# Fourteen TensorE products of a tile of ones ahead of the first real product of a fused attention and token-mixing kernel

## Chip, cores and metric

The kernel runs on one core of one Trainium2 chip. The metric is device time in microseconds. The kernel before took 584.02 us, the median of three runs (583.85, 584.02 and 584.76 us).

## What is computed

Two blocks follow one another for eight batch entries: banded attention with 8 heads of width 64 over 576 positions, then a mixing block on the 512 columns that the heads give together.

```python
scores = q @ k.T / sqrt(64)        # heads 0-3: the last 32 positions
                                   # heads 4-7: every 4th of the last 128
x = softmax(masked scores) @ v     # to [8, 576, 512]
theta = x @ w_theta
y = w_tok_r @ (x * cos(theta)) + w_tok_i @ (x * sin(theta))
u = x + y
out = u + relu(u @ w_ch)
```

## The kernel before

Heads are taken in pairs, four pairs to a batch entry. The host lays out q, k and v so that a pair's masked scores are 9 strips of 128 rows by 64 columns. For each pair, in a batch entry:

- **scores** (L441): the strips are computed in two halves, of 5 and of 4 strips, each into one of two PSUM banks tagged "s". In the first entry, L424 first writes the mask into the bank (an identity in bf16 times the mask tile), then L468 adds two f32 products of 64 columns per strip, 10 in the first half and 8 in the second (each is two rows of the trace, so x20 and x16). DVE takes the row maximum (L430) and subtracts it (L433), which frees the bank. ACT computes exp (L493), DVE the row sums (L495) and their reciprocal (L507, L508), POOL multiplies (L510).
- **flip** (L543, first entry only): TensorE transposes the probabilities (L561), DVE and ACT copy them out (L536, L539). Later entries use DVE transposes (`turn`, L525).
- **pv** (L603): probabilities times v (L617) into the bank pair tagged "v" (one buffer, 1024 f32 columns), copied out by ACT (L581).

Then `theta0` and `theta` (L667, L685) multiply by w_theta, `trig` makes sine and cosine (K L787 to cos L705) and splits the products with x into a high and a low part (L644, L646), `token` (L850) and `chan` (L882) do the two large products in three passes each, and DVE, ACT and POOL make the residuals. Weights come in packed and are unpacked by DVE and ACT (`unpack`, L332 to L342) and split by ACT and POOL (`split`, L350, L352).

What sets the order. All TensorE instructions are kept in the order in which the program writes them (the helper `pe`, L170). For the first batch entry, a planner in the kernel (class `Order`) also orders DVE, ACT, POOL and the DMA issues, with ranks and estimated costs; from L987 on (`od.live = False`, batch entries 1 to 7 of the last stages and 2 to 7 of the first) only TensorE's order is written by hand, and a scheduler at build time orders the other engines with its own simulated clock.

All loads are issued by SP in one queue. `first_loads` (L270) brings the mask and the bf16 identity, then q and k of the four pairs of the first entry with the f32 identity after pair 0, then v of the four pairs; then come w_theta (L325) and the token weights (L323, L325). `consts` (L301) sets a constant on DVE (L303) and clears two tiles on POOL (L307). In the kernel before, TensorE's first instruction is the mask product L424 of pair 0.

The last lines ahead of the planner's start, next to which the change is made:

```python
    UH = {d: reserve(f"u{d}") for d in range(NC)}
    od.live = True
    go(first_loads(), 0)
    go(consts(), 0)
```

Of the kernel before, what the change touches and what calls it, by code (L numbers as in the profile page):

```python
# [8 lines left out]
F32 = mybir.dt.float32  # L9
F32R = mybir.dt.float32r  # L10
BF16 = mybir.dt.bfloat16
# [7 lines left out]
DM = H * D  # L19
# [18 lines left out]

FG0 = {4: ("zl2", "zl6"), 0: ("zl3", "zl7"), 1: ("zh3", "zh7")}
COS_PSUM, SIN_PSUM = True, True  # L40
KORD = (0, 4, 1, 5, 2, 6, 3, 7, 8)
TP0 = {4: "s", 0: "s", 1: "x", 2: "t", 3: "s"}
TP = {4: "t", 0: "s", 1: "s", 2: "t", 3: "s"}
# [18 lines left out]
class Order:  # L62
# [20 lines left out]
    def go(self, gen, rank=None):  # L83
        if not self.live:
            for _ in gen:
                pass
            return
        self.serial += 1
        t = [self.rank if rank is None else rank, self.serial, self.now, gen, None, 0.0]
        self.tasks.append(t)  # L90
        self.advance(t)
# [60 lines left out]
def build(ctx, tc, qT, kT, vw, wth, wtk, wch, maskb, ident, identb, outT):  # L152
    nc = tc.nc
    cp = ctx.enter_context(tc.tile_pool(name="const", bufs=1))
# [7 lines left out]
    ps_v = ctx.enter_context(tc.tile_pool(name="ps_v", bufs=1, space=PSUM))  # L162
# [7 lines left out]
    def pe(ins):  # L170
        tc.keep_in_program_order(ins)
# [13 lines left out]
    def reserve(tag):  # L185
        taken[tag] = taken.get(tag, -1) + 1
        return taken[tag]

    def take(tag, bufs, n=None):
        n = reserve(tag) if n is None else n  # L190
        if od.live:
            if n >= bufs:
                yield None, ("free", tag, n - bufs)
            if n:
                yield None, ("got", tag, n - 1)
            signal(("got", tag, n))
        return n
# [5 lines left out]
    def bank(tag, name):  # L203
        if tag == "v":
            n = yield from take(tag, 1)
            return ps_v.tile([128, 2 * DM], F32, tag=tag, name=name), (tag, n)
        pl, bufs = banks[tag]
        n = yield from take(tag, bufs)
        return pl.tile([128, DM], F32, tag=tag, name=name), (tag, n)
# [60 lines left out]
    def first_loads():  # L270
        yield "DMA", dma(3 * BW + 64)
        pin(nc.sync.dma_start(mskb, maskb.bitcast(BF16)))
        pin(nc.sync.dma_start(idb, identb.bitcast(BF16)))
        for pr in range(NP):
            yield from take(f"xh{pr}", 1, 0)
            yield from take(f"u{pr}", 1, 0)
            pqs.append(hp.tile([128, 2, S], F32R, tag=f"xh{pr}", name=f"P0_{pr}").bitcast(F32)[:, 0])
            q = hp.tile([128, 2, S], F32R, tag=f"u{pr}", name=f"q0_{pr}").bitcast(F32)
            q = q.rearrange("p a b -> p (a b)").rearrange("p (a b) -> p a b", b=2 * QB)
            k = first_k[:, KE * pr:KE * pr + KE]  # L280
            yield "DMA", dma(2 * S)
            pin(nc.sync.dma_start(q, qT[0, pr]))
            yield "DMA", dma(KE)
            pin(nc.sync.dma_start(k, kT[0, pr]))
            qks[0, pr] = (q, k, None)
            if pr == 0:
                yield "DMA", dma(128)
                pin(nc.sync.dma_start(idt, ident))
            signal(("qk", 0, pr))
        for pr in range(NP // 2):  # L290
            v = first_v[:, NJ * 128 * pr:NJ * 128 * pr + NJ * 128].rearrange("p (a b) -> p a b", b=128)
            yield "DMA", dma(NJ * 128)
            pin(nc.sync.dma_start(v, vw[0, pr]))
            for h, t in (("a", v[:, :VA]), ("b", v[:, VA:])):
                vs[h, 0, pr] = (t, None)
                signal(("v" + h, 0, pr))
        for pr in range(NP // 2, NP):
            yield from load_va(pr)
            yield from load_vb(pr)
# [517 lines left out]
    def residual(b, d, g, ps, rel):  # L817
        ts = slice(HS * g, HS * g + HS)
        x = xf[b, d]
        if g == 0:  # L820
            yield from take(f"u{d}", 1, UH.get(d) if b == 0 else None)
            u = hp.tile([128, 2, S], F32R, tag=f"u{d}", name=f"u{b}_{d}")
# [10 lines left out]
    def unit_bank(b, n):  # L833
        return "mmx"[n % 3] if b else "m"

    def token(b, d, g):
        yield None, ("z", b, KORD[0])
        yield None, ("wtk", g, KORD[0] // 2)
        ps, rel = yield from bank(unit_bank(b, NC * g + d), f"y{b}_{d}_{g}")
        ps = ps[:, :HS]  # L840
        cs = slice(128 * d, 128 * d + 128)
        n = 0
        for kt in KORD:
            yield None, ("z", b, kt)
            yield None, ("wtk", g, kt // 2)
            zh, zl = zs[b, kt]
            wh, wl = (w[:, HS * (kt % 2):HS * (kt % 2) + HS] for w in wtks[g, kt // 2])
            yield "PE", 369
            for l, r in ((zh, wh), (zh, wl), (zl, wh)):
                pe(nc.tensor.matmul(ps, l[:, cs], r, start=(n == 0), stop=(n == 3 * NK - 1)))  # L850
                n += 1
        signal(("tk", b, d, g))
        go(residual(b, d, g, ps, rel), RANK["evacuate"])
# [99 lines left out]
    EA, LA, LA2 = ([(t, reserve(t)) for t in ts] for ts in (EARLY, LATE, LATE2))  # L953
    XH = {p: reserve(f"xh{p}") for p in range(NP)}
    UH = {d: reserve(f"u{d}") for d in range(NC)}
    od.live = True
    go(first_loads(), 0)
    go(consts(), 0)
# [100 lines left out]
```

## Time and profile before

| | |
|---|---|
| three runs, median | 584.02 us |
| profiled execution, its own time | 585.12 us |
| its span, first to last instruction | 583.3 us |
| mean granted TensorE clock of the span | 0.987 |
| TensorE busy | 553.4 us, 95% |
| VectorE (DVE) busy | 377.9 us, 65% |
| ScalarE (ACT) busy | 343.9 us, 59% |
| GpSimd (POOL) busy | 222.5 us, 38% |

The profiled execution took 1.8 us more than its span, for what lies around the first and the last instruction, and 1.10 us more than the median of the three runs. Busy times overlap between engines. A busy TensorE need not run at its full clock: the profile gives the clock granted by the throttle as a share, 1.00 for 2.4 GHz and 0.50 for 1.2 GHz, from the first change of the clock that it recorded.

### The profile page before, as it was taken

What the parts mean: (1) busy time and instruction counts of PE and PEld (TensorE: products, weight loads), DVE (VectorE), ACT (ScalarE), POOL (GpSimd) and SP (SyncE); (2) the same over time, 40 slices, a digit from 0 to 9 for tenths busy, and PEclk for the clock granted to TensorE, in tenths of its full rate; (3) what the DMA queues carried; (4) which work ended last, traced back from release to release, by engine and by line L of the source; (5) the groups of instructions that cost most, each with busy time, mean ns of one, the idle gap of its engine ahead of it and who ended that gap; (6) DMA issues with size and microseconds to landing.
All of it is one profiled execution on the core that took longest, in us unless ns stands there. A gap on an engine that the chain in (4) does not pass through costs nothing.

```text
span 583.3 us, 13997 instructions
## 1 busy us (share of the span) xinstructions
PE 553.4 (95%) x5464; PEld 503.5 (86%) x5464; DVE 377.9 (65%) x1156; ACT 343.9 (59%) x939; POOL 222.5 (38%) x206
## 2 busy tenths in 40 slices
PE   5997799999999899999999899998999899999997
PEld 3744698879999799988999799988999799989997
DVE  3779798866666768666765767666775667545112
ACT  1498967767554784459555695349645685267110
POOL 2227855525124362326324263225423262326120
PEclk9999699899999999999999999999999999999999
DMA  8990437601748056460746246470746323331002
GB/s 300 400 360 16 172 101 247 212 0 75 215 144 200 25 175 211 100 174 27 261 144 162 65 144 202 116 197 1 251 146 165 96 83 102 66 98 60 24 0 82
DMA packets 45586, 81.91 MB, mean 140 GB/s; under 512 B 3920, under 2 KB 19024, under 8 KB 45520
## 3 DMA queue, kind: packets, MB, share of 16 engines
q1 hardware_dynamic: 45520, 81.02, 43.9%
q8 instruction: 43, 0.70, 0.5%
q14 instruction: 23, 0.19, 0.1%
HBM read 64.49 MB, written 16.52 MB: 139 GB/s over the span
## 4 chain that ended last, share of the span: by engine, by line
DVE 31%; PE 29%; ACT 26%; POOL 6%; issue 4%; DMA 3%; SPq 1%; ACTq 0%; DVEq 0%
DVE pt L525 14%; PE y L850 13%; ACT P L504 10%; PE c L882 7%; PE th L685 4%; DVE P L409 4%; POOL zl L646 3%; DVE xh L599 2%; POOL P L510 2%; ACT zh L644 2%; ACT K L698 2%; ACT K L787 2%; PE s L468 2%; ACT cos L705 2%; ACT th L796 2%
## 5 line engine op out<-in xcount | busy, mean ns | idle before, releaser
L830 POOL TENSOR_TENSOR u<-x,u 128x288 fp32r<-128x288 f32 x64 | 54.9, 858 | 190.1 <-ACT u L828 190.1
L525 DVE STREAM_TRANSPOSE pt<-P 32x288 f32<-32x288 f32 x224 | 105.1, 469 | 12.1 <-POOL P L510 8.5
L882 PE MATMUL c<-u,late_wc 128*128 128x288 f32 x768 | 108.9, 295 | 0.0
L882 PEld LDWEIGHTS c<-u,late_wc 128*128 128x128 f32 x768 | 105.9, 188 | 2.8
L850 PE MATMUL y<-wtkh,zh 128*128 128x288 f32 x288 | 90.4, 314 | 1.8 <-ACT zh L644 1.8
L828 ACT CAST u<-x 128x288 fp32r<-128x288 f32 x64 | 27.4, 429 | 108.0 <-DVE x L825 108.0
L850 PE MATMUL y<-wtkh,zl 128*128 128x288 f32 x288 | 86.4, 300 | 4.0 <-POOL zl L646 4.0
L646 POOL TENSOR_TENSOR zl<-g,zh 128x512 fp32r<-128x512 f32 x40 | 52.6, 1317 | 94.8 <-ACT zh L644 81.9
L850 PE MATMUL y<-wtkl,zh 128*128 128x288 f32 x288 | 86.0, 299 | 0.0
L685 PE MATMUL th<-wthh,xh 128*128 128x512 f32 x224 | 75.1, 396 | 7.4 <-DVE g L748 7.4
L504 ACT ACTIVATE P<-P,mx 128x64 f32<-128x64 f32 x216 | 72.0, 335 | 10.3 <-DVE mx L498 9.6
L850 PE MATMUL y<-late_wt_b,zh 128*128 128x288 f32 x320 | 68.2, 297 | 0.0
L825 DVE TENSOR_TENSOR x<-y,x 128x288 f32<-128x288 f32 x64 | 28.6, 450 | 54.9 <-PE y L850 54.6
L850 PEld LDWEIGHTS y<-wtkh,zh 128*128 128x128 f32 x288 | 55.3, 192 | 5.3 <-ACT zh L644 2.9
L850 PEld LDWEIGHTS y<-wtkh,zl 128*128 128x128 f32 x288 | 55.3, 192 | 4.7 <-POOL zl L646 4.7
L685 PEld LDWEIGHTS th<-wthh,xh 128*128 128x128 f32 x224 | 42.0, 187 | 17.3 <-issue 8.4
L850 PE MATMUL y<-late_wt_a,zh 128*128 128x288 f32 x256 | 56.8, 304 | 0.0
L850 PEld LDWEIGHTS y<-wtkl,zh 128*128 128x128 f32 x288 | 55.3, 192 | 0.3 <-issue 0.3
L510 POOL TENSOR_TENSOR P<-P,sm 128x576 f32<-128x576 f32 x32 | 37.5, 1172 | 42.0 <-DVE sm L508 18.1
L850 PEld LDWEIGHTS y<-late_wt_b,zh 128*128 128x128 f32 x320 | 51.5, 189 | 0.3
L850 PE MATMUL y<-late_wt_b,zl 128*128 128x288 f32 x160 | 47.3, 296 | 0.0
L581 ACT COPY x<-o 128x576 f32<-128x576 f32 x32 | 29.7, 928 | 28.8 <-PE o L617 24.0
(108 smaller groups left out, 1107.6 us busy)
## 6 DMA issues: line engine op xcount, KB each, us to landing
q<-in_qT_dram SPq DMA_DIRECT2D x32, 576.0 KB, 5.1
va<-in_vw_dram SPq DMA_DIRECT2D x30, 320.0 KB, 3.4
k<-in_kT_dram SPq DMA_DIRECT2D x28, 304.0 KB, 5.7
out_dram<-x SPq DMA_DIRECT2D x28, 288.0 KB, 2.3
vb<-in_vw_dram SPq DMA_DIRECT2D x29, 256.0 KB, 3.8
xd<-xq SPq DMA_DIRECT2D x24, 288.0 KB, 5.2
xn<-xd SPq DMA_DIRECT2D x24, 256.0 KB, 5.1
st_wtk<-in_wtk_dram SPq DMA_DIRECT2D x8, 576.0 KB, 9.1
```

Of the source, the lines that this page charges most:

```text
L409: pin(nc.vector.tensor_tensor_reduce(out=P[:, n], in0=ps[:, n - g0], in1=mskb[:, mask_of(pr, n)], op0=ALU.add, op1=ALU.max, scale=1.0, sca ...
L504: table(nc.scalar.activation(P[:, n], P[:, n], AF.Exp, bias=mx[:, n:n + 1], scale=SCALE, accum_out=sm[:, n:n + 1]))
L510: pin(nc.gpsimd.tensor_tensor(P, P, sm.unsqueeze(2).to_broadcast([128, NJ, BW]), op=ALU.mult))
L525: pin(nc.vector.transpose(pmats[b, pr][k0:k0 + QB, :, hh, QB * e:QB * e + QB], P[p0:p0 + QB, :, QB * o:QB * o + QB]))
L581: pin(nc.scalar.copy(dst, src))
L646: pin(nc.gpsimd.tensor_tensor(lo, z, hi.bitcast(F32), op=ALU.subtract))
L685: pe(nc.tensor.matmul(pt, l, r, start=(n == 0), stop=(n == 3 * NC - 1)))
L825: pin(nc.vector.tensor_tensor(x[:, ts], ps, x[:, ts], op=ALU.add))
L828: pin(nc.scalar.copy(uh[b, d][:, ts], x[:, ts]))
L830: pin(nc.gpsimd.tensor_tensor(ul[b, d][:, ts], x[:, ts], uh[b, d][:, ts].bitcast(F32), op=ALU.subtract))
L850: pe(nc.tensor.matmul(ps, l[:, cs], r, start=(n == 0), stop=(n == 3 * NK - 1)))
L882: pe(nc.tensor.matmul(ps, l[:, cs], r[:, ts], start=(n == 0), stop=(n == 3 * NC - 1)))
```

## The change

A tile of ones, 128 partitions by 512 columns in bf16, is made by a DVE memset. Fourteen products of it (128 x 128 stationary, 512 columns moving) are written into the first bank of the "v" bank pair, one over the other. They are issued through `pe`, so they stand ahead of every other TensorE instruction. Nothing reads what they write. Everything else is unchanged.

```diff
+WARM_UP = 14
...
     UH = {d: reserve(f"u{d}") for d in range(NC)}
+
+    ones = cp.tile([128, DM], BF16, name="ones")
+    nc.vector.memset(ones, 1.0)
+    busy = ps_v.tile([128, 2 * DM], F32, tag="v", name="busy")
+    for n in range(WARM_UP):
+        pe(nc.tensor.matmul(busy[:, :DM], ones[:, :128], ones, start=True, stop=True))
     od.live = True
     go(first_loads(), 0)
     go(consts(), 0)
```

## Rows read from the trace of the kernel before

**Rows 1.** The page, busy time of each engine: us, share of the span, instructions.

```profile
PE 553.4 (95%) x5464; PEld 503.5 (86%) x5464; DVE 377.9 (65%) x1156; ACT 343.9 (59%) x939; POOL 222.5 (38%) x206
```

**Rows 2.** Busy time by stretch: us from:to, length, engines (instructions), clock, DMA share, GB/s.

```profile
13.38:19.10 5.72, 5.72 (x86) 4.98 (x86) 3.07 (x8) 1.10 (x2) 1.15 (x1) 1.00 1.03 404
19.10:56.00 36.90, 33.48 (x378) 19.07 (x376) 32.04 (x69) 29.17 (x51) 15.85 (x11) 1.00 0.66 252
...
120.00:580.00 460.00, 451.53 (x4313) 423.93 (x4311) 283.04 (x929) 262.55 (x722) 161.95 (x153) 1.00 0.40 120
```

**Rows 3.** The chain that ended last, 3 to 24 us: start, length, what.

```profile
3.53 6.73 DMA first_k<-in_kT_dram
...
10.40 1.35 PE s L468 x20
...
13.38 0.45 PE s L424 x5
13.83 1.27 PE s L468 x20
15.10 0.33 PE s L424 x4
15.42 1.05 PE s L468 x16
16.48 1.26 PE pT L561 x20
17.74 0.38 PE s L424 x5
18.12 1.07 PE pT L561 x16
...
21.32 0.80 PE pT L561 x20
22.11 0.22 PE s L424 x4
22.34 0.64 PE pT L561 x16
```

**Rows 4.** The timeline, 0 to 25 us: start, length, engine, line, operation, form, idle before.

```profile
0.73 2.05 POOL L307 MEMSET pt<- 128x1152 f32 x2 [0.29 <-POOLq L1045]
...
0.80 0.06 DVE L303 MEMSET halfpi<- 128x1 f32 x1 [0.80 <-PEq L1045]
...
7.79 0.49 DVE L430 TENSOR_REDUCE mx<-s 128x5 f32<-128x320 f32 x1 [6.93 <-PE s L468]
...
19.10 0.82 PE L468 MATMUL s<-first_k,q 128*64 128x64 f32 x20
...
24.41 0.91 DVE L332 TENSOR_SCALAR st_wth<-st_wth 128x512 f32<-128x512 f32 x1
```

**Rows 5.** DMA issues at 5.5 and at 11.7 us: queue, count, KB, us to landing.

```profile
first_k<-in_kT_dram SPq DMA_DIRECT2D x1, 304.0 KB, 9.2
...
st_wth<-in_wth_dram SPq DMA_DIRECT2D x1, 512.0 KB, 8.7
```

**Rows 6.** TensorE products at either clock: lines of 67.8 to 73.7, timeline of 47.

```profile
L850 PE MATMUL y<-wtkh,zl 128*128 128x288 f32 x8 | 3.7, 462 | 1.1 <-POOL zl L646 1.1
...
47.04 3.77 PE L667 MATMUL th<-st_wth,x 128*128 128x512 f32 x8
```

**Rows 7.** Busy time by stretch around the recorded changes of the clock; columns as rows 2.

```profile
56.00:60.14 4.14, 1.50 (x21) 1.11 (x20) 4.14 (x9) 3.47 (x8) 3.71 (x4) 1.00 0.63 163
60.14:63.55 3.41, 3.38 (x41) 2.96 (x42) 2.64 (x21) 3.39 (x6) 3.41 (x4) 0.50 0.86 331
63.55:66.96 3.41, 1.45 (x8) 0.99 (x8) 3.41 (x14) 3.34 (x13) 2.43 (x3) 1.00 0.71 241
66.96:73.79 6.83, 5.92 (x24) 5.92 (x25) 4.55 (x11) 6.83 (x31) 6.20 (x6) 0.50 0.03 12
...
328.00:332.00 4.00, 2.50 (x12) 1.97 (x11) 1.96 (x3) 3.89 (x8) 0.04 (x1) 1.00 0.00 0
```

## The prediction, made before the change was run

> **What bounds the kernel now.** The page comes first: TensorE is busy 95% of the span [rows 1]. Such an average mixes stages, so the busy times by stretch are read next. From 120 to 580 us TensorE is busy 451.5 of 460 us, at the full clock: that part is a queue of products, and whatever starts it earlier ends it earlier. From 19.1 to 56 us VectorE (32.0 of 36.9 us) and ScalarE (29.2) are the crowded ones, passing work to each other. From 13.4 to 19.1 TensorE is busy in every moment, with VectorE half idle [rows 2]. The third view, the chain that ended last, says who holds whom at the start: the load of pair 1's k until 10.3 us, then a chain that is TensorE almost throughout until 19.2: scores of pairs 1 and 2, their masks, the flips of pair 0 [rows 3].
>
> The reader should next compare equal work on both sides of 19.1. Twenty rows of score products take 1.35 and 1.27 us in the chain at 10.4 and 13.8, and 0.82 us at 19.10 in the timeline; the flip of 20 rows takes 1.26 at 16.5 and 0.80 at 21.3 [rows 3, 4]. Nothing but the clock differs, so TensorE runs at the lower of its two levels (1.2 GHz) until about 19.1 us and at 2.4 GHz after it. The clock column shows 1.00 before 19.1 too [rows 2]; the durations contradict it, and I go by them. Before this rise TensorE had been busy without a break for 5.7 us.
>
> **The change, part by part.** The loads don't move: SP issues them as before, and none of their queue waits for TensorE until far behind the first products.
>
> *The memset.* VectorE does one 59 ns memset at 0.80 and then nothing until 7.79 us [rows 4]. No VectorE memset of 512 columns is in the trace. The bounds are that small one, 0.06 us, and the 512-column VectorE operation at 24.41, 0.91 us; I take 0.46 us from POOL's memsets (2.05 us for two of 1152 columns, so 0.89 ns a column) [rows 4]. It is hidden, and sets when the products can begin: about 1.4 us.
>
> *Fourteen products.* No bf16 product of 512 columns is in the trace. At the lower clock 24 one-pass products of 288 columns fill 5.92 us [rows 7], 0.247 us each and 0.86 ns a column, or 0.44 us for 512. The bounds: half of that, if the clock were full at once, so 3.1 us in all; and twice the f32 row of 512 columns (8 rows in 3.77 us at the full clock, 0.47 each [rows 6]), so 0.94 at the lower and 13.2 us in all. The first is excluded for most of them, as the clock starts low; the bf16 product is one pass like the 288-column one, which is the nearer row. Fourteen take 6.1 us if all run low, and TensorE is free at about 7.5; if the clock rises on the way, at about 6.5. The Trainium skill ("TensorE: Matmul & The Clock Gate", section "Wait — 56ns, not 53.3ns?") gives 426.7 ns for such a product at the lower clock; by it the fourteen take 5.97 us.
>
> *Pair 0.* Its mask products, which ran at 3.0 us, and its scores (from 6.41 us, when k had landed) now stand behind the fourteen. They would be done by 7.5 + 0.22 + 0.82 + 0.22 + 0.64 = 9.4 us at full clock. Pair 1's k lands at 10.3 in any case [rows 3], so up to 0.9 us of lateness costs nothing.
>
> *Scores and flips at the full clock.* This is the gain, and it lies on the chain, from 10.40 to 19.2. Each low row against its equal at the full clock [rows 3, 4]: scores x20, 1.35 to 0.82 (0.53) and 1.27 to 0.82 (0.45); masks 0.45, 0.33 and 0.38 to some 0.25 each (0.41 together); scores x16, 1.05 to 0.64, taking the flip of 16 rows as its like (0.41); flip x20, 1.26 to 0.80 (0.46); flip x16, 1.07 to 0.64 (0.43). The sum is 2.69 us. Is something else late then? Pair 3's k lands at 5.5 + 9.2 = 14.7 us [rows 5], and its scores would start at 19.10 - 2.69 = 16.4. VectorE's part (row maxima, row sums) takes 3.07 of 5.72 us there [rows 2], so it follows.
>
> *Behind 19 us.* The full gain passes on if what VectorE needs next has landed. The first w_theta tile lands at 11.7 + 8.7 = 20.4 us and is first touched at 24.41 [rows 4, 5]: 4.0 us of room for a move of 2.7. From there VectorE, ScalarE and TensorE hand each other work without a landing in the chain, until the packed stretch of products begins at 67.87.
>
> *The sum.* 585.12 - 2.69 = 582.43 us for the profiled execution. That execution is 1.10 us above the median of 584.02. For the median I take less than 2.69: in a run where the first rise comes sooner than at 19.1 there is less left to win. Here the rise at 63.55 followed 3.38 us of work, and that at 73.79 followed 5.92 [rows 7]; had the first one come after 3.4 us of dense work, at 16.8, some 2.3 us at the lower clock, worth about 0.9, would be gone. A third of that off gives 2.4: **581.6 us**.
>
> **The rivals.**
>
> *The clock falls back before 19 us.* The fourteen raise it, but the real work behind them is thin: between 9.4 and 12.9 us TensorE, at full clock, would have 1.7 us of products (0.82, 0.22 and 0.64 for pair 1), then wait for VectorE to free a bank. The trace has two falls: at 60.14, after 1.50 us of work in 4.14, and at 66.96, after 1.45 in 3.41; where it had 2.50 in 4.00, at 328, the clock stayed up [rows 7]. The new gap lies between these, and if the warm-up ends at 6.5 the gap starts a microsecond earlier and looks more like the falls. Then pair 1's first half has gained its 0.53, and the dense work behind it runs low again as now. Time: 584.02 - 0.5 = 583.5. The Trainium skill ("TensorE: Matmul & The Clock Gate", section "Why this matters for your kernels") warns only against idle gaps longer than those that would be left here; by that rule the clock stays up and the time is the forecast's. The trace does not agree: before the fall at 60.14 the idle moments together were 2.64 us, so no single gap was that long.
>
> *The gain is given back later.* The low stretch from 66.96 to 73.79 lies under packed products [rows 7] and costs 5.92/2 = 3.0 us; with another start it can be shorter, as from 60.14 to 63.55, or another can appear, at half of its length each. By the same page of the skill ("What's actually happening") the chip's observation of activity runs freely and does not start with the kernel, so such stretches would lie elsewhere from run to run; one trace can't show that, the spread of 0.9 us over three runs does not contradict it. As a rival: a stretch of 3.4 us at the lower clock more than now, 1.7 us, and the time is 584.02 - 2.4 + 1.7 = 583.3. The low stretch at 67 cut to the shorter kind gives (5.92 - 3.38)/2 = 1.3 us more, 580.4. VectorE's and ScalarE's orders in the later entries, made at build time with a simulated clock, can add as much either way.
>
> *It doesn't warm.* If products of ones don't raise the clock, all is as before: 584.0. Against it: the fourteen and pair 0's scores make 6 to 9 us of work without a break, more than the 5.7 and 5.92 us that went before the rises at 19.1 and 73.79.
>
> *The products outlast the loads* (slower). If one takes more than 0.51 us, fourteen and pair 0 end later than 10.4, and pair 1 starts late. At the upper bound, 0.94, they end at 14.6; pair 0 then takes 1.9, pair 1 starts at 16.5 in place of 10.4, 6.1 us late, and 2.7 are won back: 587.4. It breaks even where the fourteen end at 11.2 us (0.70 each), 2.7 us past the point where it begins to cost. For it speaks only the f32 row, of another type.
>
> **How the numbers follow.** Forecast (clock stays up, gain carried) 0.55; falls back 0.22; given back 0.12; doesn't warm 0.05; outlasts 0.06. About 0.2% (1.2 us) is what a measurement of this kernel can tell from no change, so faster is below 582.85 and slower above 585.19. Faster: nearly all of the forecast and a little of the second, 0.56. Slower: the last, and some of the give-back with an unlucky order, 0.10. Same: 0.34. The range goes from 580.4 (a low stretch less) to 584.5 (nothing won, with the spread of the runs).
>
> **What would show it.** Fourteen rows of about 0.43 us from 1.4 us on; pair 1's first twenty score rows in about 0.82 us, still from 10.4; pair 3's first half near 16.4 in place of 19.10; the first w_theta unpack near 21.7 in place of 24.41; packed products from about 65.2 in place of 67.87. The forecast is wrong if score rows between 12 and 19 us take 1.3 us per twenty (it fell back), or if pair 1 starts later than 10.4 (it outlasts), or if 24.41 moves and 67.87 doesn't.

## The result, and the profile after

The changed kernel takes 586.17 us (median of 22 runs, 584.24 to 587.72), the kernel before 583.93 us in 22 runs beside it (582.07 to 585.59). The ratio is 1.0037, interval [1.0027, 1.0047]: the change makes the kernel slower, by 2.2 us.

All engines' instructions stand in the same order as before; added are one memset and 28 TensorE instructions (14 weight loads, 14 products). Up to the added block line numbers are one higher (L468 is now L469), behind it seven (L1045 is L1052). The profiled execution took 585.44 us, 0.73 below its median, where the one of before lay 1.19 above the median of these 22 runs: the two traces are only 0.34 us apart in span (583.66 to 583.31), and the runs of the experiments must say how much of the 2.2 us is typical.

The page's busy line of the changed kernel, against [rows 1]: TensorE is busy 1.7 us less, VectorE 1.9 us more.

```profile
PE 551.7 (95%) x5478; PEld 499.4 (86%) x5478; DVE 379.8 (65%) x1157; ACT 344.2 (59%) x939; POOL 222.7 (38%) x206
```

The timeline of the changed kernel, VectorE at the start and at the first w_theta unpack, columns as [rows 4]:

```profile
0.91 0.48 DVE L959 MEMSET ones<- 128x512 bf16 x1 [0.91 <-PEq L1052]
...
22.05 0.91 DVE L333 TENSOR_SCALAR st_wth<-st_wth 128x512 f32<-128x512 f32 x1
```

TensorE in the same view:

```profile
1.45 4.80 PE L962 MATMUL busy<-ones 128*128 128x512 bf16 x14 [1.45 <-DVE halfpi L304]
...
6.79 0.80 PE L469 MATMUL s<-first_k,q 128*64 128x64 f32 x20 [0.40 <-DMA first_k<-in_kT_dram]
...
9.90 0.80 PE L469 MATMUL s<-first_k,q 128*64 128x64 f32 x20 [0.88 <-DMA first_k<-in_kT_dram]
...
15.84 0.80 PE L469 MATMUL s<-first_k,q 128*64 128x64 f32 x20
16.47 0.86 PE L618 MATMUL o<-pt,first_v 128*64 128x64 f32 x22
18.39 0.62 PE L618 MATMUL o<-pt,first_v 128*64 128x64 f32 x14 [1.06 <-issue]
...
24.52 0.68 PE L562 MATMUL pT<-idt,P 64*64 64x64 f32 x14 [0.89 <-issue]
...
66.56 0.61 PE L851 MATMUL y<-wtkh,zl 128*128 128x288 f32 x1 [1.11 <-POOL zl L647]
```

The start does what was wanted, and more: the products end at about 6.2 us, every score row of 20 takes 0.80 us, and pair 3's first half starts at 15.84 in place of 19.10 [rows 4], 3.26 us earlier. Then two lines end in "issue": inside one run of equal products TensorE stands still for 1.06 and 0.89 us and waits for nothing that the profile shows. Before has no such line in this stretch. After both, where the packed products begin, 66.56 stands against the 67.87 of before: 1.31 us are left.

The busy times by stretch, columns as [rows 2]. The clock stayed up until 66.18 us; one low stretch of 3.42 us follows, where before has one of 3.41 and one of 6.83 [rows 7]. From 120 us on TensorE works as before, 451.18 us against 451.53 [rows 2].

```profile
4.74:15.84 11.10, 8.71 (x171) 6.46 (x169) 6.42 (x15) 1.52 (x3) 1.15 (x1) 1.00 1.01 379
66.18:69.60 3.42, 3.04 (x12) 3.04 (x13) 1.34 (x4) 3.42 (x19) 2.79 (x4) 0.50 0.00 1
120.00:580.00 460.00, 451.18 (x4311) 423.87 (x4311) 283.33 (x930) 262.58 (x722) 161.95 (x153) 1.00 0.40 120
```

The next loss lies on VectorE. First the kernel before, timeline of VectorE, 85 to 100 us:

```profile
85.12 0.49 DVE L430 TENSOR_REDUCE mx<-s 128x5 f32<-128x320 f32 x1 [0.86 <-PE s L468]
...
92.35 0.43 DVE L332 TENSOR_SCALAR st_wch<-st_wch 128x512 f32<-128x512 f32 x1
...
94.97 0.77 DVE L332 TENSOR_SCALAR st_wch<-st_wch 128x512 f32<-128x512 f32 x1 [0.74 <-DMA st_wch<-in_wch_dram]
...
96.03 0.68 DVE L342 SCALAR_TENSOR_TENSOR st_wch<-st_wch 128x512 uint32<-128x512 uint32 x1
96.63 0.21 DVE L597 TENSOR_TENSOR xh<-x,xh 128x64 fp32r<-128x64 f32 x1
...
97.73 0.69 DVE L342 SCALAR_TENSOR_TENSOR st_wch<-st_wch 128x512 uint32<-128x512 uint32 x1
...
99.97 0.95 DVE L525 STREAM_TRANSPOSE pt<-P 32x288 f32<-32x288 f32 x2
```

The same rows of the changed kernel:

```profile
83.81 0.49 DVE L431 TENSOR_REDUCE mx<-s 128x5 f32<-128x320 f32 x1 [0.86 <-PE s L469]
...
92.01 0.43 DVE L333 TENSOR_SCALAR st_wch<-st_wch 128x512 f32<-128x512 f32 x1 [1.20 <-DMA st_wch<-in_wch_dram]
...
93.80 0.38 DVE L333 TENSOR_SCALAR st_wch<-st_wch 128x512 f32<-128x512 f32 x1
...
94.46 1.28 DVE L343 SCALAR_TENSOR_TENSOR st_wch<-st_wch 128x512 uint32<-128x512 uint32 x1
95.66 0.82 DVE L598 TENSOR_TENSOR xh<-x,xh 128x64 fp32r<-128x64 f32 x1
96.40 0.94 DVE L526 STREAM_TRANSPOSE pt<-P 32x288 f32<-32x288 f32 x2
97.38 1.00 DVE L343 SCALAR_TENSOR_TENSOR st_wch<-st_wch 128x512 uint32<-128x512 uint32 x1
...
99.91 0.95 DVE L526 STREAM_TRANSPOSE pt<-P 32x288 f32<-32x288 f32 x2
```

And POOL beside them, changed kernel:

```profile
93.96 1.23 POOL L511 TENSOR_TENSOR P<-P,sm 128x576 f32<-128x576 f32 x1 [3.11 <-DVE sm L509]
95.31 1.09 POOL L831 TENSOR_TENSOR u<-x,u 128x288 fp32r<-128x288 f32 x1
96.52 1.31 POOL L353 TENSOR_TENSOR late_wc<-st_wch,late_wc 128x512 fp32r<-128x512 f32 x1
```

At 85 us the changed kernel is 1.31 us ahead (83.81 to 85.12), at 100 us 0.06. VectorE's wait has moved from the second st_wch tile (0.74 us) to the first (1.20 us), ahead of the rows that release POOL. So POOL's L511 starts just ahead of VectorE's L343 and no longer while VectorE waits: L343 takes 1.28 us for 0.68, L598 0.82 for 0.21, the next L343 1.00 for 0.69, 1.52 us together, each beside a POOL row. The transposes L526, with one input, take 0.94 beside POOL as ever. The Trainium skill ("SBUF — State Buffer", section "Who interferes with whom") says that a VectorE instruction with two inputs in SBUF and a GpSimd one that reads SBUF exclude each other, the later being held until the first ends. The trace agrees: L511 ends at 95.19, and L343 ends 0.55 us later, at 95.74; the second L343 ends 0.55 us behind POOL's L353 too (98.38 and 97.83).

Why does the first tile come late? The chain that ended last, changed kernel, goes through its load:

```profile
85.99 5.92 DMA st_wch<-in_wch_dram
...
92.01 0.43 DVE st_wch L333
```

Before, the same load was issued at 87.31 and landed at 92.25, in 4.94 us. The one thing found that differs within it is a packet of the instruction queue. Its row in the DMA view (queue, packets, MB, share of 16 engines) of 88.7 to 88.8 us, changed kernel:

```profile
q8 instruction: 1, 0.02, 55.7%
```

The page lists 43 packets and 0.70 MB on that queue, 16.3 KB each, for before and after. Spread over TensorE's 10,956 instructions that is 64 bytes each and 256 to a packet; and the kernels below with 256 TensorE instructions more have 44 packets. So TensorE's instructions come by DMA while it works. The Trainium skill ("Runtime: NRT & Kernel Launch", section "Terms") says that an engine's instruction memory is refilled in 16 KiB blocks; the trace agrees. Twenty-eight instructions more move every later packet to an earlier product. In the changed kernel the packet starts at 88.74, 2.75 us after the load's issue; before at 91.63, 4.32 us after it. The theory to be tested: **the added instructions, not the warm-up, cost the time, through the place of these transfers.** Rivals: the warm start itself brings a bad order or longer stretches at the lower clock; or every added instruction costs.

### The profile page after: what moved, and what is told of

It reads as the page before. It is cut to its first block, busy times and chain, and to the rows that moved or that the text cites. A ratio compares the mean times of both kernels' runs of the same rounds, so it can differ in the third digit from the quotient of the medians.

```text
span 583.7 us, 14026 instructions
## 1 busy us (share of the span) xinstructions
PE 551.7 (95%) x5478; PEld 499.4 (86%) x5478; DVE 379.8 (65%) x1157; ACT 344.2 (59%) x939; POOL 222.7 (38%) x206
## 4 chain that ended last, share of the span: by engine, by line
DVE 33%; PE 27%; ACT 27%; POOL 5%; issue 4%; DMA 2%; SPq 0%; ACTq 0%; DVEq 0%; POOLq 0%
DVE pt L526 16%; PE y L851 11%; ACT P L505 10%; PE c L883 7%; PE th L686 4%; DVE P L410 4%; POOL zl L647 3%; DVE xh L600 2%; POOL P L511 2%; ACT zh L645 2%; ACT K L699 2%; ACT K L788 2%; ACT cos L706 2%; PE s L469 2%; ACT th L797 2%
## 5 line engine op out<-in xcount | busy, mean ns | idle before, releaser
L526 DVE STREAM_TRANSPOSE pt<-P 32x288 f32<-32x288 f32 x224 | 105.1, 469 | 12.0 <-POOL P L511 8.5
L505 ACT ACTIVATE P<-P,mx 128x64 f32<-128x64 f32 x216 | 72.0, 335 | 10.3 <-DVE mx L499 9.7
L511 POOL TENSOR_TENSOR P<-P,sm 128x576 f32<-128x576 f32 x32 | 37.6, 1175 | 41.4 <-DVE sm L509 18.8
```

Of the source, the lines that this page charges most:

```text
L505: table(nc.scalar.activation(P[:, n], P[:, n], AF.Exp, bias=mx[:, n:n + 1], scale=SCALE, accum_out=sm[:, n:n + 1]))
L511: pin(nc.gpsimd.tensor_tensor(P, P, sm.unsqueeze(2).to_broadcast([128, NJ, BW]), op=ALU.mult))
L526: pin(nc.vector.transpose(pmats[b, pr][k0:k0 + QB, :, hh, QB * e:QB * e + QB], P[p0:p0 + QB, :, QB * o:QB * o + QB]))
```

## The experiments

Each ratio is to the kernel before, run beside it on the same chip. "Packet" is the start of the instruction packet near 90 us counted from the issue of the first st_wch load, "load" that load's time to landing.

**Both kernels again.**

> The kernel before, unchanged, for a second trace and more times. All theories: 584 us. Theory A (stalls and hand-over): no idle moment of TensorE over 0.8 us between 13 and 30 us that ends without a wait. Theory B (low-clock stretches): fewer low stretches of the clock behind 120 us than in the changed kernel, so a higher mean clock (0.987 or more).

> The changed kernel, unchanged, for a second trace. All theories: about 586. Theory A: TensorE again idle near 17.3 and 23.6 us, about 1 us each, without a wait, whatever the times of the clock's changes. Theory B: its low stretches lie elsewhere than in the first trace, and their number goes with the time, 1.7 us for each of 3.4 us that lies on packed products.

Before again: 584.41 us, ratio 0.9997 [0.9980, 1.0013]; packet 4.27, load 4.74. Changed again: 586.60, 1.0041 [1.0027, 1.0056]; packet 2.55, load 5.90, the same two stalls (1.06 and 0.89 us), and L343 and L598 at 1.27, 0.82 and 1.01. The trace of before again has two things new: pair 1's k landed half a microsecond sooner, and the clock rose sooner, in the middle of pair 0's flip (timeline, TensorE):

```profile
9.89 1.34 PE L468 MATMUL s<-first_k,q 128*64 128x64 f32 x20 [0.20 <-DMA first_k<-in_kT_dram]
...
14.85 1.12 PE L468 MATMUL s<-first_k,q 128*64 128x64 f32 x16
15.90 1.04 PE L561 MATMUL pT<-idt,P 64*64 64x64 f32 x20
16.87 0.32 PE L424 MATMUL s<-mskb,idb 128*128 128x64 bf16 x5
17.12 0.68 PE L561 MATMUL pT<-idt,P 64*64 64x64 f32 x16
```

The two together put it 1.39 us ahead of the first trace of before at 90 us, without a stall: as far as the changed kernel gets. Of this, 0.51 us is k (pair 1's scores start at 9.89 in place of 10.40) and 0.86 comes with the rise (pair 3's first half starts at 17.73 in place of 19.10). Between these two repeats the spans differ by 1.77 us: 0.22 at 90 us, 1.45 more from 90 to 101, 0.10 behind.

**The same 28 instructions without warming** (tiny14).

```diff
-        pe(nc.tensor.matmul(busy[:, :DM], ones[:, :128], ones, start=True, stop=True))
+        pe(nc.tensor.matmul(busy[:, :8], ones[:, :128], ones[:, :8], start=True, stop=True))
```

> Fourteen products of 8 columns in place of 512: the same count of instructions, too little work to raise the clock. Theory A: first rise near 17 to 19 us as before, no stall without a wait at 17 to 25 us (the lower clock asks for instructions more slowly), time that of before, 584. Theory B: 584 too. Theory C (28 more TensorE instructions shift the whole stream, whatever they do): 586.

587.28 us, 1.0054 [1.0035, 1.0073]: slower than before, and no faster than the change, though the clock rises only at about 19.8 us and there are no stalls. Packet 2.92, load 6.04; L343 1.27, L598 0.82, L343 1.02. So the loss near 95 us needs no warm start.

**Half of the products** (seven). `WARM_UP = 7`.

> Seven products of 512 columns in place of fourteen: they end near 4.5 us, two microseconds ahead of the first q and k. Theory A: if the clock is up by 7 us, stalls as in the changed kernel and 586; if it isn't, 584. Theory B: between. Theory C: half of the shift, 585.

584.78 us, 1.0013 [0.9999, 1.0026]. The clock rose at 4.7, fell again at 8.1 and rose at 18.4: pair 1's scores take 1.34 us again, so this is the rival in which it falls back. Packet 4.14, load 4.72, no loss on VectorE.

**A whole packet of instructions more** (tiny128). `WARM_UP = 128`, products of 8 columns (256 instructions).

> 128 products of 8 columns, 256 TensorE instructions more in place of 28, ending near 6.4 us by the 0.54 us that fourteen took, ahead of the first q and k; too little work to raise the clock. Theory A' (what costs is where TensorE's 16 KB instruction transfers fall against the loads of w_ch, and 256 instructions further on they fall where they fell before): the first st_wch load takes 4.7 to 4.9 us, not 5.9 to 6.0, VectorE does not lose 1.5 us between 94 and 99 us, and the time is 584.4 to 585. Theory C (each further instruction costs): 588 or more.

585.00 us, 1.0004 [0.9994, 1.0014]; packet 4.24, load 4.74. Nine times as many further instructions as in tiny14 cost nothing that this measurement can tell: the rival by which each costs falls.

**The same 256, wide enough to warm** (cols48). `WARM_UP = 128`, products of 48 columns.

> 128 products of 48 columns: 256 instructions and some 5.5 to 6 us of work at the lower clock. Theory A': as the last, and if the clock rises by 8 us, 1.3 us less at 30 us than the kernel before, kept to the end: 583.3. Without that rise 584.4. The stalls without a wait, 257 TensorE rows apart, lie 28 rows later in the work than with fourteen products. Theory C: 588 or more.

584.22 us, 0.9991 [0.9976, 1.0005]. Inconclusive as to a gain: the clock rose at 5.5, fell at 12.3, after a wait of 2.39 us for pair 1's k, and rose at 19.1. Packet 4.09, load 4.57.

That late k is a second place where a packet and a long load go together. In these two kernels with 256 instructions more at the start, the first packet comes at 7.46 us (128 products of 8 columns) and at 9.23 us (of 48), inside the load of pair 1's k, which takes 7.84 and 8.00 us from issue to landing. In the other eleven traces no packet lies inside it, and it takes 6.17 to 6.93 us. The DMA view at 3.5 us, products of 48 columns first, then the change:

```profile
first_k<-in_kT_dram SPq DMA_DIRECT2D x1, 304.0 KB, 8.0
...
first_k<-in_kT_dram SPq DMA_DIRECT2D x1, 304.0 KB, 6.2
```

**Ten products** (ten). `WARM_UP = 10`.

> Ten products of 512 columns (20 instructions), ending near 5.4 us. Theory A': clock up at 5 to 8 us, gain of 3 us at 20 us, 2 of it lost in stalls; then it is the first st_wch load that decides: 4.8 us long, 583.5; 6.0 us long, 586. Theory C: 0.7 of the loss of fourteen, 586.

584.82 us, 1.0002 [0.9991, 1.0012]; packet 3.90, load 4.67. The early rise did not come: the first one recorded is at 17.3 us, pair 1's scores take 1.34 us, and pair 3's first half starts at 18.50, a gain of 0.6 us and not of 3. Stalls all the same, of 0.48 and 0.91 us, at 20.6 and 26.7, in other products than in the change.

**Seven products, later, without the memset** (late7), of the bf16 identity, behind its landing.

```diff
+WARM_UP = 7
...
+        busy = ps_v.tile([128, 2 * DM], F32, tag="v", name="busy")
+        for n in range(WARM_UP):
+            pe(nc.tensor.matmul(busy[:, :DM].rearrange("p (a b) -> p a b", b=128), idb,
+                                idb.unsqueeze(1).to_broadcast([128, 4, 128]), start=True, stop=True))
```

> Seven products of 512 columns of the bf16 identity, right behind its landing: 3.0 to 6.0 us, with no memset and no product earlier, so that the scores at 6.6 follow at once. Theory A': 14 instructions as in the kernel with seven products, so no loss at 94 to 99 us; clock up by 9 us and staying, 3 us less at 20 us, 1.2 less at 30 us, 583.3 in all. If the clock falls again before 18 us, 584.4. Theory C: 585.

584.29 us, 0.9997 [0.9988, 1.0005]. They run from 3.15 to 6.3; the clock stays up and pair 3's first half starts at 15.84, as in the change. Packet 4.08, load 4.77, no loss at 95 us. But the stalls are there, 0.87 and 0.90 us. The full warm start, without the loss at 95 us, is worth nothing that this measurement can tell.

**The phase of the packets alone: 14 small products at 28 us** (mid14), in a kernel whose start is that of before.

```diff
             yield "PE", 860
+            if c == 0 and st == STS[0]:
+                for _ in range(14):
+                    pe(nc.tensor.matmul(ths[0, st][0][:, :8], idb, idb[:, :8], start=True, stop=True))
             pe(nc.tensor.matmul(ths[0, st][0][:n], xf[0, c][:, cs], wth32[c],
```

> The kernel before with 14 products of 8 columns at about 27 us (written into the first theta bank ahead of its first real product): 28 more TensorE instructions, and the first 27 us as before. If the phase of the instruction transfers matters: the transfer at 91.6 us of the kernel before starts about 2.7 us after the issue of the first st_wch load, that load takes about 6 us in place of 4.9, VectorE loses about 1.5 us at 94 to 99 us, and the time is 585.8 to 587, ratio about 1.003 to 1.005. If only the start matters: as before, 584.4, ratio 1.000.

586.56 us, 1.0038 [1.0021, 1.0055]: the whole loss, without any warm-up. Packet 2.79, load 5.90. VectorE is level with before at 90 us (0.02) and 1.30 us behind at 101. Its timeline:

```profile
93.36 0.43 DVE L332 TENSOR_SCALAR st_wch<-st_wch 128x512 f32<-128x512 f32 x1 [1.18 <-DMA st_wch<-in_wch_dram]
...
95.81 1.27 DVE L342 SCALAR_TENSOR_TENSOR st_wch<-st_wch 128x512 uint32<-128x512 uint32 x1
97.01 0.82 DVE L597 TENSOR_TENSOR xh<-x,xh 128x64 fp32r<-128x64 f32 x1
...
98.73 1.00 DVE L342 SCALAR_TENSOR_TENSOR st_wch<-st_wch 128x512 uint32<-128x512 uint32 x1
...
111.67 1.05 DVE L438 TENSOR_SCALAR mx<-mx 128x4 f32<-128x4 f32 x1
```

The last line is the rest: a row of four elements that takes 0.17 us in the trace of before takes 1.05 beside a POOL row (0.72 in the changed kernel, at 110.33, and 1.26 in changed again), and from there mid14 is 2.0 us behind to the end.

**The change, filled up to a whole packet.** 114 products of 8 columns behind the fourteen (pad114), or ahead of the first token product (realign).

```diff
+    for n in range(114):
+        pe(nc.tensor.matmul(busy[:, :8], ones[:, :128], ones[:, :8], start=True, stop=True))
```

```diff
-        ps = ps[:, :HS]
+        pad, ps = ps[:, DM - 8:], ps[:, :HS]
...
+            if (b, d, g, kt) == (0, 0, 0, 0):
+                for _ in range(114):
+                    pe(nc.tensor.matmul(pad, ones[:, :128], ones[:, :8], start=True, stop=True))
```

> The change with 114 products of 8 columns behind its fourteen, so that 256 TensorE instructions more than in the kernel before are issued in all, and the 16 KB instruction transfers fall at the same products as before. The small ones end near 9.4 us, before pair 1's k lands. If the place of the instruction transfers against the st_wch loads costs the 1.5 us at 94 to 99 us: that loss is gone (the first st_wch load takes 4.6 to 4.9 us again, VectorE's L343 0.7 us), and the time is 584.4 or less, ratio at most 1.000. If the stalls of TensorE without a wait at 18 and 24 us go too: about 583. If a warm start by itself (not the instruction count) does the harm, or every further instruction costs: 586 to 587, ratio 1.003 or more.

> The change with 114 products of 8 columns ahead of the first token product (near 60.6 us, into columns that nothing reads): 256 TensorE instructions more than before in all, but the first 60 us as in the change. They take about 3.2 us, of which about 2.6 fall into TensorE's wait there. If the phase of the instruction transfers near 90 us costs the 1.5 us: it is gone, and the time is 584.2 to 585.0, ratio 0.9995 to 1.001. If not: 586 to 587.

pad114: 584.77 us, 1.0014 [0.9997, 1.0032]; packet 4.04, load 4.73. realign: 585.23, 1.0012 [0.9997, 1.0027]; packet 3.95, load 4.60. In both L343 is back at 0.68 and L598 at 0.20 and 0.21: the loss near 95 us is gone from the traces, with the warm start still there. The times alone would not show it, since both intervals reach that of the change. Neither reaches a gain. In pad114 the clock fell at 9.1 us, under the small products, though TensorE had no gap, and pair 0's scores took 1.34 us again. In realign the small products ran at 49.2 us, not near 60.6 us as expected. The stalls remain (1.04 and 1.16 us), the clock is low from 24.9 to 28.3 us, the start's 3.3 us are down to 0.6 by 28 us, and 0.77 go at 105 to 109 us, where the fourth st_wch tile took 6.06 us. The same load took 6.03 in before again and 5.30 in the first trace of before: such a loss befalls runs of before too.

## Why the prediction was wrong

*The start was right, with half a microsecond of luck.* Memset: 0.46 forecast, 0.48 measured. Products: about 0.43 apart at the lower clock, and the clock rose at 4.74, so the fourteen end at about 6.2 us (6.5 forecast for that case). Pair 3's first half moves by 3.26 us, forecast 2.69. But 0.50 of it is pair 1's k, which the prediction held to land at 10.3 "in any case": here its scores start at 9.90, and in before again, without any change, at 9.89. From there to pair 3's first half the change takes 5.94 us for 8.70 before: a gain of 2.76 us, where the sum of the prediction had 2.69.

*"Behind 19 us: the full gain passes on" failed.* The 67.87 was to become 65.2 and became 66.56. The sum looked at landings that VectorE needs and left out one supply, TensorE's own instructions. The two stalls last 1.95 us together; the lead goes from 3.26 us to 1.17 at the first theta product (26.92, before 28.09) and is 1.31 at 66.56. In the five traces that have them (the change twice, late7, ten, realign) they stand at the same two places of TensorE's instruction stream, 449 and 706 rows from the first with its waits counted, 257 apart, whatever product lies there, and a packet starts 2.4 to 2.6 us ahead of their ends (15.89 and 22.12 us in the change). That the faster stretch overtakes the supply is the reading that fits: in all thirteen traces TensorE runs neither row sooner than 2.38 us after the start of the last packet, and the eight without the first stall come to row 449 3.3 us or more after it. In pad114 the second is hidden in a wait: POOL's L511 ends at 21.04, and TensorE goes on at 21.70, 2.38 us after a packet. No run tests this reading by itself.

*The carry from 67.87 to the end failed.* The prediction has no loss behind 67.87 and no term for the added instructions themselves. In the trace pair the account closes: 3.26 gained, 1.95 gone by 66.56, 1.25 between 85 and 100 us around the first st_wch load, 0.40 behind (most of it at L439), so 0.34 us slower, which is the difference of the spans. With fourteen products too small to warm anything the kernel is slower all the same (tiny14, 1.0054).

*The correction for an earlier first rise had the right price.* The prediction put 0.9 us on a rise at 16.8 in place of 19.1; before again has its first recorded rise at 16.5 and gains 0.86 by it. That only a third of this was to be taken off was a guess, and the landing of k, worth another 0.51 there, was not in the sum. Against such a run nothing is left of the start: at 66 us both are 1.31 us ahead of the first trace of before. Two traces don't tell how often that is so. That the warm start without the loss near 95 us and without a fall of the clock, though with the stalls (late7), is worth 0.9997 fits it.

*What makes it slower* is the number of added instructions and, by all that the runs show, the place of the instruction packets that goes with it. Of the thirteen traces, the four with 28 instructions more (the change twice, tiny14, mid14) have the packet 2.55 to 2.92 us after the issue, the load at 5.90 to 6.04 and ratios of 1.0037 to 1.0054; all with 0, 14, 20 or 256 more have it 3.90 to 4.32 after, the load at 4.57 to 4.94, and ratios of 0.9991 to 1.0014. Moving the instructions behind the start (mid14) keeps the loss, filling up to a packet removes it; in time this is clear of noise for tiny14 against tiny128 and for mid14 against before. Longer stretches at the lower clock do not carry it: the mean granted clock of the runs is 0.989 in tiny14 and 0.990 in tiny128, 2.3 us apart, and lowest, 0.983, in seven, at 1.0013. Nor does a bad order, as the order is that of before. How one packet of 16 KB lengthens a load of 512 KB by 1.1 us is not shown; only that the two go together. The packet's row above, 55.7% of 16 engines for 0.1 us, is 0.89 us of one DMA engine, so an estimate from it is of the right size if a part of the load waits behind the packet; that it does is not shown.

*The rivals.* "Given back later" (583.3 us) was the nearest in kind, but by another mechanism than low stretches: between 60 and 74 us the change has 6.8 us less of them. What a shorter stretch is worth shows on TensorE, the change first, then before:

```profile
80.73 0.29 PE L851 MATMUL y<-wtkh,zl 128*128 128x288 f32 x1
82.24 0.31 PE L425 MATMUL s<-mskb,idb 128*128 128x64 bf16 x5 [1.22 <-ACT P L486]
...
83.33 0.29 PE L850 MATMUL y<-wtkh,zl 128*128 128x288 f32 x1
83.55 0.31 PE L424 MATMUL s<-mskb,idb 128*128 128x64 bf16 x5
```

Its lead has grown from 1.31 to 2.60 us, near the 1.3 more that the prediction gave for a shorter stretch; then it waits for ACT, and 1.31 are left. So at 82 us the products are not yet a queue in which what starts earlier ends earlier, and the 580.4 at the low end of the range rested on a gain that does not pass on. "Falls back" came true in seven and cols48, not in the change. "Outlasts" and "doesn't warm" fell. No rival held a loss that comes from the number of instructions, so the range ended at 584.5.

## What to carry to other kernels

Adding instructions to an engine moves its later instruction transfers, so a change at the start can cost time far behind it; test it with the same number of instructions that do nothing, and with a full packet of them (256 here), before the change itself is blamed. Look for waits marked "issue" inside runs of equal products: where a stretch of short products gets faster, its instruction supply can be the next bound. And compare with several traces of the kernel before, since what a warm-up is to win may already be won in some of its runs.

## What the runs showed of the hardware that was not expected

- TensorE stood still for 0.48 to 1.16 us at rows 449 and 706 of its stream in five traces; in none of the thirteen did it run these rows sooner than 2.38 us after the start of a 16 KB instruction packet.
- The first 512 KB load of st_wch took 4.57 to 4.94 us where such a packet started 3.90 to 4.32 us after its issue, and 5.90 to 6.04 us where it started 2.55 to 2.92 us after. The 304 KB load of pair 1's k took 6.17 to 6.93 us without a packet in it, 7.84 and 8.00 with one.
- VectorE rows beside POOL rows: 0.68 to 1.28 us, 0.21 to 0.82, and 0.17 to 1.26 for a row of four elements.
- The clock fell under 114 products of 8 columns that followed each other without a gap (9.1 us in pad114), and as such a row of them ended (52.2 us in realign).
